# Down slabs split earlier, normalised rows on ScalarE, the inverse spread to the end, and four banks for the last four down blocks

## The chip, the cores and the metric

The kernel runs on one core of a Trainium2 chip. The metric is the device time of one execution in microseconds (us). The core has a matrix engine (TensorE, PE in the profile), two engines for element-wise work (VectorE, DVE, and ScalarE, ACT), GpSimd (POOL), and SyncE (SP), which here issues all transfers. Each engine works through its own instruction order and waits on semaphores for the others. Matrix products are written to PSUM, which has eight banks per partition; an element-wise engine has to read a bank out before it can be used again.

## The reference

`x` is 2048 x 448. Its rows are normalised, and the result is the sum of three things: `x` itself, a filter in the frequency domain, and a gated feed-forward block with 1792 hidden columns.

```python
xn = _layernorm(x, axis=-1)                       # (x - mean) / sqrt(var + 1e-5)
# A: X = rfft2(xn) * (w_r + 1j * w_i);  y = irfft2(X)
# B: gate = xn @ W_gate; up = xn @ W_up
#    h = gate * (gate > 0) * up;  y = h @ W_down
return x + _A_ref(xn, A_w_r, A_w_i) + _B_ref(xn, B_W_gate, B_W_up, B_W_down)
```

## The kernel before

**Numbers in two parts.** TensorE multiplies f16 numbers. Every f32 operand is therefore split in two f16 parts, a high and a low one, after scaling, and a product is made of three: high by high, high by low, low by high. ACT makes the high part (a scaled copy) and DVE the low one (the operand minus the high part). This holds for the normalised rows, the weights, the hidden values `h` and the operands of the Fourier transforms.

**Rows and chunks.** The 2048 rows are 16 tiles `n2` of 128; the four tiles with the same `n2 % 4` are a chunk `q` of 512 rows. The chunks are taken in the order 0, 2, 1, 3.

**The feed-forward block sets PE's order.** The 1792 hidden columns are 14 slabs `f` of 128, in groups of 5, 5 and 4. For each group, each chunk and each slab there is a gate/up unit `("gu", g, f, q)`: 20 matmuls of 512 columns and two half passes, into two banks of the tile `gu`, of which there are two, so four banks in all. Then `gu_post` reads it out in four operations that alternate between ACT and DVE: `gu_relu` (line 765), `gu_times` (769), which is the last to read the banks, `gu_hi` (773) and `gu_lo` (777). When a group's slabs are done for a chunk, four down units `("dn", g, n2)` follow, one for each tile of rows: `dn_mm` (796) runs three matmuls of 448 columns for each slab into one of two banks `dn`, and `dn_post` (802) adds the scaled result to `xy`, where the output is gathered. Down units are placed a little after their chunk, behind the next pair of gate/up units. The last four have nothing behind which to stand and come at the very end.

**The slabs of the weights** are prepared on the way. For a down slab these are `load_wd`, `wd_sq` (squares, ACT, line 186), `wd_sum` (sum over partitions, POOL), `wd_scale` (ten tiny DVE operations, up to line 706), `wd_hi` (ACT, 710) and `wd_lo` (DVE, 714). `sched(gslot(s, n), ...)` hangs them on the unit that is `n` gate/up units ahead of `s`, the last gate/up unit before the group's first down block.

**The background.** The Fourier work and the normalisation of chunks 1 and 3 form one list `bg` with a cost in us of DVE for each step. `run_bg` hands out steps while there is credit; each unit brings as credit a share of its time less what it costs DVE itself (`room`). The share is found by halving an interval so that the credit of the units from `RAMP` to `last_gu` is just the list's cost. The normalisation of a tile in the list is `ln_norm`: `ln_xn` (290) makes the row, `ln_hi` (299) its high part, `ln_copy` moves pieces, and `ln_lo` follows. The inverse transform is the end of the list: per tile `i_swap`, `i_pair`, `i_quad` (599 to 604), `i_hi` (611), `i_lo` (617), `i_sdft` (PE, 627), `i_pq` (632), `i_pqlo` (636), `i_ddft` (PE, 646) and `i_acc` (651), which adds to `xy`. Its two products use the two banks `fx`.

**The order of the instructions.** Apart from the opening, whose order is written out by hand, a scheduler puts each engine's instructions in order ahead of the run: among those that are ready in its own reckoning it takes the one with the highest priority. Priority is the order in the program, raised for `gu_post` and `dn_post` (by 400) and for the weights (by 200). On the chip an engine keeps that order, so an instruction that has to wait holds those behind it. A tile of rows is stored when both its sums are in: `store` acts at its second call.

Of the kernel before, what the change touches and what calls it, by code (L numbers as in the profile page):

```python
# [10 lines left out]
F32 = mybir.dt.float32  # L11
BF16 = mybir.dt.bfloat16
U32 = mybir.dt.uint32
AF = mybir.ActivationFunctionType
OP = mybir.AluOpType
AX = mybir.AxisListType

S, D, F = 2048, 448, 1792
# [5 lines left out]
GROUPS = [5, 5, 4]  # L24
# [120 lines left out]
def tile_gfnet_reglu(ctx: ExitStack, tc: tile.TileContext, x, xr, wgu, wd, wf, ident, c_fd, c_fm, c_im, c_row, c_id,  # L145
                     out):
    nc = tc.nc
    V, A, P, G = nc.vector, nc.scalar, nc.tensor, nc.gpsimd

    main = ctx.enter_context(tc.tile_pool(name="main", bufs=1))  # L150
    psum = ctx.enter_context(tc.tile_pool(name="psum", bufs=1, space=bass.MemoryType.PSUM))

    def mt(shape, dt, name, bufs=1):
        return main.tile(shape, dt, name=name, bufs=bufs)
# [6 lines left out]
    ov = out.rearrange("(n p) d -> p n d", n=16)  # L161
    wdv = wd.rearrange("(f p) d -> f p d", p=128)

    xy = mt([128, 16, D], F32, "xy")
# [11 lines left out]
    dsc = mt([128, len(GROUPS)], F32, "dsc")  # L176
# [33 lines left out]
    xr_t, xr_b = {}, {}  # L210
# [44 lines left out]
    rst = {}  # L255
# [19 lines left out]
    xn, tt, xn_b = {}, {}, {}  # L275
# [7 lines left out]
        tt[n2] = tts[state.setdefault("tn", 0) % 4]  # L283
        state["tn"] += 1

    def ln_xn(n2):
        xn_b[n2] = free.pop(0)
        xn[n2] = xn_b[n2].rearrange("p g c k -> p (g c k)")[:, 0:D]
        r, _, mean = rst[n2 % 4, n2 // 4]
        V.tensor_scalar(xn[n2], xr_t[n2], mean, r, op0=OP.subtract, op1=OP.mult)  # L290

    def ln_hi(n2, fused=False):
        new_tt(n2)
        o = tt[n2].rearrange("p a b -> p (a b)")[:, 0:D]
        r, nm, _ = rst[n2 % 4, n2 // 4]
        if fused:
            A.activation(o, xr_t[n2], AF.Identity, scale=r, bias=nm)
        else:
            A.activation(o, xn[n2], AF.Copy)  # L299

    def ln_copy(n2):
        t = tt[n2]
        G.tensor_copy(t[:, 7, 0:48].rearrange("p (a b) -> p a b", b=16), t[:, 0:3, 112:128])  # L303
        G.tensor_copy(t[:, 7, 64:128], t[:, 3, 0:64])

    def ln_norm(n2):
        ln_xn(n2)
        ln_hi(n2)
        ln_copy(n2)
        free.append(xr_b.pop(n2))  # L310
# [344 lines left out]
    wt, wdt, wsc = {}, {}, {}  # L655
# [61 lines left out]
    hps, ht = {}, {}  # L717
# [25 lines left out]
    def gu_unit(f, q, mate):  # L743

        gs, cs = (0, 1), slice(0, 512)
        if (f, q) in opened:
            gu_full(f, q, gs, cs, False, True)
            return
        gu_open(f, q)
        gu_full(f, q, gs, cs, True, False)  # L750
        gu_halves(f, q, mate)
# [33 lines left out]
    dps = {}  # L785
    stored = set()

    def dn_mm(fs, n2):
        q, j = n2 % 4, n2 // 4
        js = slice(128 * j, 128 * (j + 1))  # L790
        ps = psum.tile([128, 512], F32, name="dn", bufs=2)
        n = 3 * len(fs)
        i = 0
        for f in fs:
            for a, b in ((0, 0), (0, 1), (1, 0)):
                last["P"] = P.matmul(ps[:, 0:D], ht[f, q][:, a, js], wdt[f][:, b, :], start=(i == 0),  # L796
                                     stop=(i == n - 1)).ins
                i += 1
        dps[n2] = ps

    def dn_post(g, n2):
        last["V"] = V.scalar_tensor_tensor(xy[:, n2, :], dps[n2][:, 0:D], dsc[:, g:g + 1], xy[:, n2, :],  # L802
                                           op0=OP.mult, op1=OP.add).ins

    def store(n2):

        if n2 in stored:
            nc.sync.dma_start(ov[:, n2, :], xy[:, n2, :])
        stored.add(n2)
# [7 lines left out]
    def add(cost, fn, *a):  # L817
        bg.append((cost, PE_US.get(fn.__name__, 0.0), fn, a))

    def ln_chunk(q):  # L820
        for j in range(4):
            add(0.79, ln_stats, q, j)
        add(0.0, ln_sd, q)
        add(0.7, ln_rstd, q)
        n = [q + 4 * j for j in (0, 2, 1, 3)]
        for t in range(4 + 2):
            for st, (c, fn) in reversed(list(enumerate(((0.51, ln_norm), (0.78, ln_lo), (0.0, ln_dma))))):
                i = t - st
                if 0 <= i < 4:
                    add(c, fn, n[i])  # L830
        marks["T", q] = len(bg)
# [108 lines left out]
    def bg_item(fn, a):  # L940

        if "P" in last:
            with tc.issue_after(last["P"]):
                fn(*a)
        else:
            fn(*a)

    def run_bg(until=None, amount=0.0):
        credit[0] += amount
        while pos[0] < len(bg) and (credit[0] > 0 if until is None else pos[0] < until):  # L950
            c, p, fn, a = bg[pos[0]]
            bg_item(fn, a)
            pos[0] += 1
            credit[0] -= c - load[0] * p


    groups, f0 = [], 0
# [4 lines left out]
    units, pend = [], []  # L962
# [17 lines left out]
    def sched(i, fn, *a):  # L980
        at.setdefault(max(i, -1), []).append((fn, a))

    gus = [i for i, u in enumerate(units) if u[0] == "gu"]
    gpos = {i: n for n, i in enumerate(gus)}

    def gslot(i, back):
        n = gpos[i] - back
        return gus[n] if n >= 0 else -1

    for f in groups[1] + groups[2]:  # L990
        s = first[f]
# [15 lines left out]
    for g, fs in enumerate(groups):  # L1007
        s = max(i for i in gus if i < first["dn", g])
        if g:
            for i, f in enumerate(fs):  # L1010
                sched(gslot(s, 4), wd_sq, i, f)
            sched(gslot(s, 4), wd_sum, len(fs))
            sched(gslot(s, 3), wd_scale, g, fs)
            for i, f in enumerate(fs):
                sched(gslot(s, 2 - i // 2), wd_hi, i, f)
                sched(gslot(s, 2 - i // 2), wd_lo, i, f)
            for i, f in enumerate(fs):
                sched(gslot(s, 14 - i), load_wd, f)

# [17 lines left out]
    for c, q in enumerate(CHUNKS[:2]):  # L1037
# [3 lines left out]
        for j in range(4):  # L1041
            n2 = q + 4 * j
# [7 lines left out]
    q = CHUNKS[0]  # L1050
# [50 lines left out]
        return max(0.0, share * took(units[i]) - fixed(i))  # L1101


    last_gu = max(gus) - 6
    lo, hi = 0.3, 1.2
    for _ in range(40):
        m = (lo + hi) / 2
# [5 lines left out]
    @contextmanager  # L1113
    def after(i):
        k = max(0, len(anchors) - 1 - i)
        with tc.issue_after(anchors[k]), tc.issue_after(act_anchors[k]):
            yield

    for i, u in list(enumerate(units))[len(groups[0]):]:
        is_gu = u[0] == "gu"  # L1120
        if is_gu:
            _, g, f, q = u
            run_bg(until=marks["T", q])
            gu_unit(f, q, (mates.get(u) or (0, 0, None, None))[2:])
        else:
            _, g, n2, _ = u
            dn_mm(groups[g], n2)
        with after(LAG):
            for fn, a in at.get(i, []):
                with tc.high_priority(offset=200):  # L1130
                    fn(*a)
            for v in units[i + 1:i + 1 + AHEAD]:
                if v[0] == "gu":
                    run_bg(until=marks["T", v[3]])
            run_bg(amount=room(i, load[0]) if i >= RAMP else 0.0)
        if is_gu:
            with tc.high_priority(offset=400):
                gu_post(f, q)
        else:
            with tc.high_priority(offset=400):  # L1140
                dn_post(g, n2)
            if g == len(groups) - 1:
                store(n2)
        anchors.append(last["V"])
        act_anchors.append(last["A"])
    run_bg(until=len(bg))


_ORDER = ["x", "xr", "wgu", "wd", "wf", "ident", "c_fd", "c_fm", "c_im", "c_row", "c_id"]
# [43 lines left out]
```

## Time and profile before

| | |
|---|---|
| median of 3 runs | 452.71 us (451.13 to 453.31) |
| the profiled execution | 451.96 us, span 450.2 us |
| PE busy | 437.9 us (97%) |
| DVE busy | 390.3 us (87%) |
| ACT busy | 181.4 us (40%) |
| POOL busy | 30.8 us (7%) |
| DMA | 39.54 MB, mean 88 GB/s |

The span runs from the first to the last instruction; the execution's own time holds 1.8 us more. Busy PE means that a matmul is in flight; matmuls overlap, so the time of one in a row is longer than its distance to the next. In a row of the timeline stand start, duration, engine, line, operation, output and inputs, shapes and how many alike follow each other; in brackets at the end stands the idle time before it and what ended that.

### The profile page before, as it was taken

What the parts mean: (1) busy time and instruction counts of PE and PEld (TensorE: products, weight loads), DVE (VectorE), ACT (ScalarE), POOL (GpSimd) and SP (SyncE); (2) the same over time, 40 slices, a digit from 0 to 9 for tenths busy, and PEclk for the clock granted to TensorE, in tenths of its full rate; (3) what the DMA queues carried; (4) which work ended last, traced back from release to release, by engine and by line L of the source; (5) the groups of instructions that cost most, each with busy time, mean ns of one, the idle gap of its engine ahead of it and who ended that gap; (6) DMA issues with size and microseconds to landing.
All of it is one profiled execution on the core that took longest, in us unless ns stands there. A gap on an engine that the chain in (4) does not pass through costs nothing.

```text
span 450.2 us, 7332 instructions
## 1 busy us (share of the span) xinstructions
PE 437.9 (97%) x2613; PEld 218.1 (48%) x2613; DVE 390.3 (87%) x963; ACT 181.4 (40%) x390; POOL 30.8 (7%) x77
## 2 busy tenths in 40 slices
PE   6999999999999999999999999999998999999996
PEld 2544644455555444444444444444454555655642
DVE  5999798968979898999999999998999997987432
ACT  5896233632455583153133533244244243134120
POOL 3220020500000120000000100000000000000000
PEclk9999999999999999999999999999999999999999
DMA  7828994400001452340320300002020211111202
GB/s 251 320 67 244 326 336 93 78 18 22 2 1 66 136 183 72 93 145 21 103 64 4 90 31 1 1 1 72 28 78 28 83 45 50 66 55 34 103 21 82
DMA packets 37612, 39.54 MB, mean 88 GB/s; under 512 B 16534, under 2 KB 33480, under 8 KB 37576
## 3 DMA queue, kind: packets, MB, share of 16 engines
q1 hardware_dynamic: 37576, 39.09, 27.9%
q8 instruction: 20, 0.33, 0.3%
q14 instruction: 16, 0.13, 0.1%
HBM read 24.38 MB, written 3.67 MB: 62 GB/s over the span
## 4 chain that ended last, share of the span: by engine, by line
PE 54%; DVE 35%; DMA 5%; issue 3%; ACT 1%; SPq 1%; DVEq 0%; ACTq 0%
PE gu L728 28%; PE dn L796 16%; DVE g L769 3%; DMA sw<-y 3%; DVE h L777 3%; DVE xy L802 2%; PE fx L358 2%; PE fx L627 2%; DVE y L500 2%; PE fx L395 2%; DVE y L499 2%; PE fx L646 2%; DVE y L401 2%; DVE y L402 2%; PE gu L735 2%
## 5 line engine op out<-in xcount | busy, mean ns | idle before, releaser
L728 PE MATMUL gu<-T,wt 128*128 128x512 f16 (+1 forms) x1140 | 254.8, 375 | 0.5 <-DVE g L769 0.5
L728 PEld LDWEIGHTS <-wt 128*128 128x128 f16 x1140 | 108.8, 98 | 129.1 <-issue 9.2
L796 PE MATMUL dn<-wdt,h 128*128 128x448 f16 x672 | 136.6, 352 | 0.9 <-DVE xy L802 0.6
L796 PEld LDWEIGHTS <-h 128*128 128x128 f16 x672 | 65.1, 98 | 63.1 <-issue 2.3
L765 ACT ACTIVATE g<-gu 128x512 f32<-128x512 f32 x56 | 33.1, 590 | 83.3 <-PE gu L735 55.7
L773 ACT ACTIVATE h<-g 128x512 f16<-128x512 f32 x56 | 35.0, 626 | 65.7 <-DVE g L769 65.6
L769 DVE SCALAR_TENSOR_TENSOR g<-gu,g 128x512 f32<-128x512 f32 x56 | 38.3, 684 | 8.1 <-ACT g L765 8.0
L777 DVE TENSOR_TENSOR h<-g,h 128x512 f16<-128x512 f32 x56 | 38.3, 685 | 5.8 <-ACT h L773 5.4
L802 DVE SCALAR_TENSOR_TENSOR xy<-dn,dsc,xy 128x448 f32<-128x448 f32 x48 | 32.4, 679 | 10.5 <-PE dn L796 10.5
L678 ACT ACTIVATE wt<-wst,wsc 128x512 f16<-128x512 f32 x28 | 19.1, 714 | 14.0 <-DVE wsc L196 14.0
L611 ACT ACTIVATE vt<-y,fsc 128x456 f16<-128x456 f32 x16 | 10.7, 669 | 26.2 <-issue 8.9
L682 DVE SCALAR_TENSOR_TENSOR wt<-wst,wsc,wt 128x512 f16<-128x512 f32 x28 | 20.4, 743 | 0.1
L189 POOL PARTITION_ALL_REDUCE wm<-wm x15 | 8.1, 539 | 169.1 <-ACT junk L186 163.6
L735 PE MATMUL gu<-T,wt 64*128 64x512 f16 x112 | 17.0, 381 | 1.7 <-DVE g L769 1.6
L186 ACT ACTIVATE junk<-wst 128x512 bf16<-128x512 f32 x28 | 17.4, 620 | 0.6 <-DMA wst<-in_wgu 0.5
L532 DVE TENSOR_TENSOR y<-y,sw 128x228 f32<-128x228 f32 x32 | 12.4, 389 | 5.0 <-DMA sw<-y 3.6
L651 DVE SCALAR_TENSOR_TENSOR xy<-fx,fsc,xy 128x448 f32<-128x448 f32 x16 | 10.8, 679 | 6.8 <-PE fx L646 6.7
L402 DVE TENSOR_TENSOR y<-y,y 128x456 f32<-128x456 f32 x22 | 13.9, 630 | 2.8 <-DMA row<-y 2.2
L386 ACT ACTIVATE Xh<-X 128x456 f16<-128x456 f32 x16 | 9.3, 578 | 15.6 <-DVE X L384 10.9
L401 DVE TENSOR_TENSOR y<-y,y 128x456 f32<-128x456 f32 x22 | 13.8, 628 | 0.3
L627 PE MATMUL fx<-im,vt 128*128 128x128 f16 x192 | 13.4, 219 | 0.7 <-DVE pgh L636 0.7
L303 POOL COPY tt<-tt 128x48 f16<-128x48 f16 x16 | 9.5, 591 | 56.4 <-ACT tt L299 51.1
(122 smaller groups left out, 458.1 us busy)
## 6 DMA issues: line engine op xcount, KB each, us to landing
sw<-y SPq DMA_DIRECT2D x64, 112.2 KB
wst<-in_wgu SPq DMA_DIRECT2D x28, 256.0 KB
wf<-in_wf SPq DMA_DIRECT2D x16, 228.0 KB
y<-in_xr SPq DMA_DIRECT2D x16, 224.0 KB
xy<-in_x SPq DMA_DIRECT2D x16, 224.0 KB
out<-xy SPq DMA_DIRECT2D x16, 224.0 KB
wdst<-in_wd SPq DMA_DIRECT2D x14, 224.0 KB
fm<-in_c_fm SPq DMA_DIRECT2D x4, 256.0 KB
```

Of the source, the lines that this page charges most:

```text
L401: V.tensor_tensor(t, a, b, op=OP.add)
L402: V.tensor_tensor(b, a, b, op=OP.subtract)
L627: P.matmul(o, v[:, h, w], m[:, c, :], start=(i == 0), stop=(i == 2), skip_group_check=True)
L682: V.scalar_tensor_tensor(w[:, 4:8, :], st, sc, w[:, 0:4, :], op0=OP.mult, op1=OP.subtract)
L728: last["P"] = P.matmul(hps[f, q][:, g, cs], wt[f, g][:, a, :], Tq[q][:, b, cs], start=(start and i == 0), stop=(stop and i == len(seq) - 1 ...
L735: m = P.matmul(hps[f, q][:, g, 0:512], wt[f, g][rows, 7, :], Tq[q][rows, b, :], start=start, stop=not start).ins
L765: last["A"] = A.activation(g1s[f, q], hps[f, q][:, 0, :], AF.Relu, scale=2.0 ** -22).ins
L769: last["V"] = V.scalar_tensor_tensor(g1, hps[f, q][:, 1, :], 2.0 ** -22, g1, op0=OP.mult, op1=OP.mult).ins
L773: A.activation(ht[f, q][:, 0, :], g1s[f, q], AF.Copy)
L777: V.tensor_tensor(h[:, 1, :], g1s.pop((f, q)), h[:, 0, :], op=OP.subtract)
L796: last["P"] = P.matmul(ps[:, 0:D], ht[f, q][:, a, js], wdt[f][:, b, :], start=(i == 0), stop=(i == n - 1)).ins
L802: last["V"] = V.scalar_tensor_tensor(xy[:, n2, :], dps[n2][:, 0:D], dsc[:, g:g + 1], xy[:, n2, :], op0=OP.mult, op1=OP.add).ins
```

## The change

Five edits.

1. **Down slabs.** Squares and sum go from 4 to 8 gate/up units ahead of `s`, the scales from 3 to 6, and the splits from two slabs per unit at 2, 1 and 0 units ahead to one slab per unit at 5, 4, 3, 2 and 1 ahead.
2. **Normalised rows.** In the background (eight tiles, chunks 1 and 3) `ln_xn` runs on ACT as one activation with scale and bias. `ln_rstd` makes the bias there, one tiny DVE operation for each chunk. The costs in the list follow: 0.51 becomes 0, 0.7 becomes 0.75.
3. **The inverse.** `last_gu`, up to which credit is counted, goes from six to two units ahead of the last gate/up unit.
4. **The last four down blocks** leave the loop. `dn_tail` takes four banks, the two `dn` and the two `fx`, runs the matmuls of all slabs but the last for all four blocks, then those of the last slab.
5. **The last block** has the matmuls of its last slab, its sum and its store in two halves of 224 columns.

```diff
-    def ln_xn(n2):
+    def ln_xn(n2, act=False):
         xn_b[n2] = free.pop(0)
         xn[n2] = xn_b[n2].rearrange("p g c k -> p (g c k)")[:, 0:D]
-        r, _, mean = rst[n2 % 4, n2 // 4]
-        V.tensor_scalar(xn[n2], xr_t[n2], mean, r, op0=OP.subtract, op1=OP.mult)
+        r, nm, mean = rst[n2 % 4, n2 // 4]
+        if act:
+            A.activation(xn[n2], xr_t[n2], AF.Identity, scale=r, bias=nm)
+        else:
+            V.tensor_scalar(xn[n2], xr_t[n2], mean, r, op0=OP.subtract, op1=OP.mult)
...
     def ln_norm(n2):
-        ln_xn(n2)
+        ln_xn(n2, True)
...
+    def dn_tail(fs, ns):
+
+        ps = [psum.tile([128, 512], F32, name="dn", bufs=2) if i < 2 else fx() for i in range(4)]
+        cut = [(slice(0, D),)] * 3 + [(slice(0, D // 2), slice(D // 2, D))]
+        for end, p, n2, cs in [(False, p, n2, cut[0]) for p, n2 in zip(ps, ns)] + [(True, *e) for e in zip(ps, ns, cut)]:
+            q, j = n2 % 4, n2 // 4
+            js = slice(128 * j, 128 * (j + 1))
+            for c in cs:
+                for f in fs[-1:] if end else fs[:-1]:
+                    for a, b in ((0, 0), (0, 1), (1, 0)):
+                        P.matmul(p[:, c], ht[f, q][:, a, js], wdt[f][:, b, c],
+                                 start=(not end and f == fs[0] and a + b == 0), stop=(end and a == 1),
+                                 skip_group_check=True)
+            dps[n2] = p
+        for n2, cs in zip(ns, cut):
+            for c in cs:
+                V.scalar_tensor_tensor(xy[:, n2, c], dps[n2][:, c], dsc[:, len(GROUPS) - 1:len(GROUPS)], xy[:, n2, c],
+                                       op0=OP.mult, op1=OP.add)
+                nc.sync.dma_start(ov[:, n2, c], xy[:, n2, c])
...
-        add(0.7, ln_rstd, q)
+        add(0.75, ln_rstd, q, (0, 1, 2, 3), True)
...
-            for st, (c, fn) in reversed(list(enumerate(((0.51, ln_norm), (0.78, ln_lo), (0.0, ln_dma))))):
+            for st, (c, fn) in reversed(list(enumerate(((0.0, ln_norm), (0.78, ln_lo), (0.0, ln_dma))))):
...
             for i, f in enumerate(fs):
-                sched(gslot(s, 4), wd_sq, i, f)
-            sched(gslot(s, 4), wd_sum, len(fs))
-            sched(gslot(s, 3), wd_scale, g, fs)
+                sched(gslot(s, 8), wd_sq, i, f)
+            sched(gslot(s, 8), wd_sum, len(fs))
+            sched(gslot(s, 6), wd_scale, g, fs)
             for i, f in enumerate(fs):
-                sched(gslot(s, 2 - i // 2), wd_hi, i, f)
-                sched(gslot(s, 2 - i // 2), wd_lo, i, f)
+                sched(gslot(s, 5 - i), wd_hi, i, f)
+                sched(gslot(s, 5 - i), wd_lo, i, f)
...
-    last_gu = max(gus) - 6
+    last_gu = max(gus) - 2
...
-    for i, u in list(enumerate(units))[len(groups[0]):]:
+    for i, u in list(enumerate(units))[len(groups[0]):-4]:
...
     run_bg(until=len(bg))
+    dn_tail(groups[-1], [u[2] for u in units[-4:]])
```

## The prediction

> **What bounds the kernel now.** I read the page first, then who TensorE (PE) waits for, then the timeline around each wait, and last the busy time of each engine by stretches.
>
> ```profile
> span 450.2 us, 7332 instructions
> PE 437.9 (97%) x2613; PEld 218.1 (48%) x2613; DVE 390.3 (87%) x963; ACT 181.4 (40%) x390; POOL 30.8 (7%) x77
> ```
> ```profile
> PE gu L735 <- DVE g L769: 1.6, 1, 1.6
> PE fx L627 <- DVE pgh L636: 0.7, 1, 0.7
> PE fx L329 <- DVE tt L314: 0.6, 2, 0.4
> PE dn L796 <- DVE xy L802: 0.6, 1, 0.6
> PE fx L329 <- ACT wt L678: 0.5, 1, 0.5
> PE gu L728 <- DVE g L769: 0.5, 1, 0.5
> PE dn L796 <- ACT wdt L710: 0.3, 1, 0.3
> ```
>
> The second fence is the list of PE's waits (who, for whom, us in total, times, longest). PE is busy 97% of the span, so a change can win only the pauses left in its stream: 4.8 us in these rows, 1.1 of them (L329) in the opening, which the change leaves alone. The question is which of the others it ends and what new ones it makes.
>
> ```profile
> 275.00:325.00 50.00, 49.54 (x247) 22.47 (x246) 47.59 (x117) 17.16 (x33) 2.19 (x3) 1.00 0.06 19
> ...
> 375.00:431.00 56.00, 56.00 (x457) 32.87 (x455) 41.34 (x90) 15.52 (x27) 0.00 (x0) 1.00 0.19 65
> ```
>
> The columns are stretch, length, then PE, PE's weight loads, VectorE (DVE), ScalarE (ACT), POOL. From 275 to 325 us DVE is full as well (47.59 of 50 us); from 375 us it has air. A small thing put into DVE's or ACT's order in the middle can therefore reach PE; at the end it hardly can.
>
> **The down slabs, the largest term.** This is the second split, that of group 2, in the timelines of ACT, DVE and PE, and last the first split in PE's.
>
> ```profile
> 334.77 2.35 ACT L710 ACTIVATE wdt<-wdst,wds 128x448 f16<-128x448 f32 x4 [6.03 <-DVE wds L706]
> 337.03 0.57 ACT L765 ACTIVATE g<-gu 128x512 f32<-128x512 f32 x1
> ```
> ```profile
> 335.52 2.46 DVE L714 SCALAR_TENSOR_TENSOR wdt<-wdst,wds,wdt 128x448 f16<-128x448 f32 x4
> 337.90 0.68 DVE L769 SCALAR_TENSOR_TENSOR g<-gu,g 128x512 f32<-128x512 f32 x1
> ```
> ```profile
> 327.17 4.48 PE L728 MATMUL gu<-T,wt 128*128 128x512 f16 x20
> 331.48 0.83 PE L627 MATMUL fx<-im,vt 128*128 128x128 f16 x12
> 332.15 4.48 PE L728 MATMUL gu<-T,wt 128*128 128x512 f16 x20
> 336.47 0.61 PE L646 MATMUL fx<-idc_t,pgh 114*128 114x112 f16 x9
> 338.64 0.61 PE L735 MATMUL gu<-T,wt 64*128 64x512 f16 x4 [1.56 <-DVE g L769]
> ...
> 340.46 0.73 PE L627 MATMUL fx<-im,vt 128*128 128x128 f16 x10 [0.74 <-DVE pgh L636]
> ```
> ```profile
> 191.63 0.54 PE L796 MATMUL dn<-wdt,h 128*128 128x448 f16 x2 [0.34 <-ACT wdt L710]
> ```
>
> The unit whose 20 matmuls began at 327.17 was done at 331.65, and its relu (L765) could have run. But ACT works in order, and ahead of the relu stood the split (L710), which waited 6.03 us for the scales, ten tiny operations that DVE threads into its full order. Then came four slabs at once on ACT (2.35 us) and on DVE (2.46 us), and the product that frees the bank (L769) ran only at 337.90. PE, through with the next unit's 20 matmuls and nine of the inverse at 337.08, stood still, and again at 340.46 for the inverse, whose DVE work had slipped behind the same burst. At 191 us a down block waited for its slab itself.
>
> A row of idle understates the loss: the 20 matmuls of 432.15 (rows of the end, below) are shown as 4.49 us, though the next matmul starts 4.33 us later, so 0.16 us goes on top of each. The three waits are 0.34 + 1.56 + 0.74 + 3 x 0.16 = 3.12 us. After the change the squares and scales stand four and three gate/up units earlier, and the slabs go one per unit, five to one units ahead of the first block, not two per unit and two to none ahead. A single slab puts 0.65 us in ACT's order and 0.68 in DVE's, against 2.35 and 2.46. No instruction is added. Three things move along. The squares (four or five on ACT) now share units with the gate/up slabs' squares and splits; ACT has 17.16 of 50 us busy there, so I price them at nothing, but a relu behind them would be held as one was behind the splits. The sum over partitions on POOL moves with them; POOL is 7% busy. And with eight slab buffers, five of them live, the last slabs must wait for the old group's last four blocks, which stand before them in the order. The waits of 191 us and of 336 us lose their cause: I take the whole 3.12 us, bounds 0 and 3.12.
>
> **Normalised rows on ACT.** Eight rows move; rows by form:
>
> ```profile
> L290 DVE TENSOR_SCALAR y<-y,mv,rs 128x448 f32<-128x448 f32 x16 | 7.6, 507 | 0.1
> ...
> L297 ACT ACTIVATE tt<-y,rs 128x448 f16<-128x448 f32 x4 | 3.0, 748 | 1.0 <-DVE rs L271 1.0
> ...
> L271 DVE SCALAR_TENSOR_TENSOR rs<-mv,rs 128x2 f32<-128x2 f32 x2 | 0.3, 160 | 0.1
> ```
>
> DVE loses 8 x 0.507 and gains two bias products of 0.16: 3.7 us less busy. ACT gains 8 operations with scale and bias, 0.748 each as in L297: 6.0 us. They fall behind the opening and before the first split of 191 us, where no wait of the list above stands, so the path gets 0; if ACT's extra time did reach PE it would cost up to 6.0 us, if DVE were the bound there it would gain up to 3.7. New is that the ACT row waits for DVE's bias with the relus queued behind it, where before the copy of the row waited for L290 in the same place.
> The Trainium skill (ScalarE: Activation LUTs, Rules for kernel authors) says that add and multiply belong on VectorE, not ScalarE. The rows agree on the single operation (507 against 748 ns); by that rule the sum would be worse by the difference.
>
> **The inverse spread to the end.** The loop that spends the credit can be gone through with its own costs. The background's cost falls from 282.0 to 278.0 (8 x 0.51 out, 2 x 0.05 in), the units that share it gain one gate/up and three down units, and the share falls from 1.081 to 1.048: some 3% less DVE work per unit in the full stretch. One wait there has only DVE's load as cause:
>
> ```profile
> 292.57 3.61 PE L728 MATMUL gu<-T,wt 128*128 128x512 f16 x16 [0.46 <-DVE g L769]
> ```
>
> It is 0.46 + 0.16 = 0.62 us; I take half, 0.3, bounds 0 and 0.62.
> The price is at the end.
>
> ```profile
> 409.27 0.67 DVE L651 SCALAR_TENSOR_TENSOR xy<-fx,fsc,xy 128x448 f32<-128x448 f32 x1
> ...
> 430.05 1.27 DVE L651 SCALAR_TENSOR_TENSOR xy<-fx,fsc,xy 128x448 f32<-128x448 f32 x2 [1.64 <-PE fx L646]
> ```
>
> In the plan the last steps of the inverse were handed out after unit 92 and now after unit 96. From 409.27 to 430.05 its last sums (L651) come in four steps, 5.2 us each, since each waits for one of two fx banks. By the plan the row that stood at unit 91 moves to 93 and the next from 92 to 95: two steps later, so the last sum falls near 430.7 + 10.4 = 441.1 on the old clock.
>
> **The four banks.** PE's and DVE's timelines of the end, and the store's issue on SP (ns):
>
> ```profile
> 432.15 4.49 PE L728 MATMUL gu<-T,wt 128*128 128x512 f16 x20
> 436.48 4.70 PE L796 MATMUL dn<-wdt,h 128*128 128x448 f16 x24
> 441.76 4.70 PE L796 MATMUL dn<-wdt,h 128*128 128x448 f16 x24 [0.59 <-DVE xy L802]
> ```
> ```profile
> 441.03 1.27 DVE L802 SCALAR_TENSOR_TENSOR xy<-dn,dsc,xy 128x448 f32<-128x448 f32 x2 [1.65 <-PE dn L796]
> ...
> 446.50 0.69 DVE L802 SCALAR_TENSOR_TENSOR xy<-dn,dsc,xy 128x448 f32<-128x448 f32 x1 [1.59 <-PE dn L796]
> ```
> ```profile
> L808 SPq DMA_DIRECT2D out<-xy x16: 332/335/457, 350.3 to 447.2; - x16
> ```
>
> The old tail has one wait, 0.59 us for a dn bank. The new one runs 36 matmuls of the first three slabs, then 9 of the last slab for three blocks and 6 of half width (half the time, an estimate). One of full width takes (4.70 - 0.16)/24 = 0.189 us. So 45 x 0.189 + 6 x 0.10 = 9.1 us from 436.48: PE's last matmul starts at 445.5, and DVE, which follows with 0.61 us per block, does the last half (0.4 us, an estimate: little over half of 0.69) by 446.75 instead of 447.19. Gain 0.4 us. Bounds 0 and 0.6. The store and the close behind it take 450.2 - 447.19 = 3.0 us and are kept: SP issues five stores for four, 0.34 us each at 0.6 us of spacing, so none queues. The last unit's halves (four operations, near 2.9 us) hide behind the 36 matmuls, 6.8 us.
> Two of the four banks are the inverse's. Its two late steps bring their own matmuls behind the last gate/up unit: 12 of L627 at 0.67 us (331.48 to 332.15) and 36 of L646 at 0.05 each (nine in 0.61 less 0.16), 2.5 us, so that unit ends near 434.0; with 18 matmuls in the dn banks PE has work until 439.9, and the first fx bank is free near 441.1. That is a pause of up to 1.2 us, unless six matmuls of the last slab (1.1 us) are ordered ahead: I take 0.5.
> The Trainium skill (PSUM — Partial Sum Buffer, PSUM bank collisions raise a hardware error) asks to guard by bank, not by address; by that the first half of the last block is not read while the second is written, and the halves gain on DVE and the store alone, as summed above. No run here shows it.
>
> **Sum.** -3.12 - 0.3 - 0.4 + 0.5 = -3.3 us on the profiled execution's 451.96 (span 450.2 and 1.8 around it): 448.7. That execution lies 0.75 us under the median of 452.71, so the forecast is **449.4 us**.
>
> **Rivals.** First, the block on ACT comes back in the new place. Scales and first slab are still one unit apart, and the scales now share DVE with two gate/up slab halves per unit. With one slab the product would come 3.1 us (the wait from 331.65 to 334.77), 0.65, 0.57 and 0.68 us after the matmuls' end, 5.0 us and more after it, where PE needs it within 5.4 (331.65 to 337.08): just in time. If the scales come 1 us later at each of the two places, 2.1 us are lost again: 451.5. For it: DVE's 47.59 of 50; against: three units of lead. Chance 0.20.
> Second, on the other side: the inverse ends too late. After the last sum PE still has two blocks, 18 + 3 matmuls and 6 halves, 4.55 us, then 1.1 for DVE and 3.0 to the span's end. Each further step of 5.2 us beyond 441.1 is lost nearly whole: one makes 449.4 + 5.2 = 454.6, two some 459. It decides from about 446 us on the old clock. For it: the plan's end moves four units, over 11 us of PE; against: DVE has 41.34 of 56 us busy there, and an idle PE shortens the steps. Chance 0.14.
> Third, ACT's longer rows reach PE: 8 x (0.748 - 0.507) = 1.9 us, 451.3. Against: no wait there. Chance 0.04. The Trainium skill's rule above would have this case.
> Fourth, the change does not do what it says: the instruction order is made by priorities among what is ready, and the slabs could be placed late all the same: 452.7. Chance 0.05.
>
> **How the numbers follow.** The forecast has 0.57; its own range is 447.0 (the median less 3.12 + 0.62 + 0.4, and less the 1.6 us by which the lowest run lies under it) to 450.4. Faster by over 0.5% (about what a measurement of this kernel can tell from no change, here 2.3 us) is this case; within 0.5% are the first, third and fourth rivals, 0.29; slower is the second, 0.14. Upwards the range takes in the fourth rival with the 0.6 us by which the highest run lies over the median, 453.4; what is left out is the second rival and little below.
>
> **What would show it.** Right: no wait of PE for L710, L735 or L627 in the middle, L710 in single rows from about 165 and 308 us on, PE waits beyond the start under 2 us, last L651 at 436 to 439, the final matmuls without a pause over 1 us. Wrong: a relu that stands behind a split for over 5 us, PE idle before the third bank, or new waits of PE between 60 and 175 us.

## The result and the profile after

| | before | after |
|---|---|---|
| median | 451.71 us (6 runs beside the after, 451.13 to 453.31) | 449.12 us (6 runs, 448.19 to 449.44) |
| ratio to before | | 0.9929 [0.9911, 0.9947] |
| profiled execution | 451.96 us, span 450.2 us | 449.44 us, span 447.6 us |

The change makes the kernel faster by 0.7% [0.5%, 0.9%]; the medians lie 2.6 us apart. The forecast was 449.4 us. The experiments below show that the total came out as forecast while three of its terms did not. Executions at a granted TensorE clock of 0.994 to 0.996 took longer (the kernel before 452.21 to 454.04 us, against 450.48 to 452.48 at 0.998 to 1.000), so a median also depends on how many of each it holds.

The page of the kernel after, then who PE waits for:

```profile
span 447.6 us, 7353 instructions
PE 437.9 (98%) x2616; PEld 218.8 (49%) x2616; DVE 387.2 (87%) x958; ACT 186.7 (42%) x398; POOL 28.8 (6%) x77
```
```profile
PE dn L1049 <- POOL warm L1106: 3.6, 1, 3.6
PE gu L738 <- DVE g L772: 1.4, 1, 1.4
PE fx L332 <- ACT wt L681: 0.4, 1, 0.4
PE dn L799 <- DVE xy L805: 0.3, 1, 0.3
PE gu L738 <- DVE wt L685: 0.2, 1, 0.2
```

Lines up to the row's stand three further down in this kernel (L772 is the product that was L769, L805 was L802, L738 the half passes of L735), the matmuls and sums of the new tail are L818 and L824. The 3.6 us for POOL belong to the opening and stand in every kernel here; the prediction's list leaves them out. The waits for the slab (L710) and for the inverse (L627) are gone. Left in the middle are 1.4 us for a product and 0.3 us for a down bank. The 1.4 us are not a new place: counted through PE's matmuls, the half passes that wait at 336.16 are the same ones that waited 1.56 us at 338.64 in the kernel before. What holds their product up is another thing now. The stretches (length, then PE, weight loads, DVE, ACT, POOL):

```profile
275.00:325.00 50.00, 49.71 (x248) 22.69 (x247) 46.60 (x117) 20.69 (x43) 1.75 (x3) 1.00 0.06 19
375.00:431.00 56.00, 56.00 (x437) 31.85 (x435) 45.12 (x104) 16.82 (x29) 0.00 (x0) 1.00 0.19 63
```

DVE has 1.0 us less in the middle (46.60 against 47.59) and 3.8 us more late (45.12 against 41.34): the inverse has moved. The slabs on ACT are single rows, and the relu waits for PE's matmuls, not behind a split:

```profile
159.10 0.66 ACT L713 ACTIVATE wdt<-wdst,wds 128x448 f16<-128x448 f32 x1
...
182.66 0.67 ACT L713 ACTIVATE wdt<-wdst,wds 128x448 f16<-128x448 f32 x1 [5.06 <-PE dn L799]
...
326.32 0.65 ACT L713 ACTIVATE wdt<-wdst,wds 128x448 f16<-128x448 f32 x1
330.21 0.60 ACT L768 ACTIVATE g<-gu 128x512 f32<-128x512 f32 x1 [3.23 <-PE gu L731]
```

The pause of the half passes in DVE's timeline, then in PE's:

```profile
315.92 0.40 DVE L535 TENSOR_TENSOR y<-y,sw 128x228 f32<-128x228 f32 x1 [2.65 <-DMA y<-row]
...
329.45 0.40 DVE L535 TENSOR_TENSOR y<-y,sw 128x228 f32<-128x228 f32 x1 [1.42 <-DMA sw<-y]
...
331.57 0.67 DVE L717 SCALAR_TENSOR_TENSOR wdt<-wdst,wds,wdt 128x448 f16<-128x448 f32 x1
...
335.43 0.68 DVE L772 SCALAR_TENSOR_TENSOR g<-gu,g 128x512 f32<-128x512 f32 x1
```
```profile
336.16 0.61 PE L738 MATMUL gu<-T,wt 64*128 64x512 f16 x4 [1.40 <-DVE g L772]
```

The relu was done at 330.81, but the product that frees the bank began at 335.43. DVE was busy all that time: it works its list in order, and between 330.67 and 335.43 stand 13 operations of the inverse, one down sum and one split (L717). It came to them late because it had stood still for 2.65 and 1.42 us, both times for a DMA: the transformed row that the inverse's pairs need, and the swapped copy. Between the row's last step and this first use stands one DVE operation; in the kernel before there stood four. What the row's wait is made of is shown below, under "Spread and rows".

### The profile page after: what moved, and what is told of

The parts are those of the page before. It is cut to its first block, busy times and chain, and to the rows that moved or that the text cites. A ratio compares the mean times of both kernels' runs of the same rounds, so it can differ in the third digit from the quotient of the medians.

```text
span 447.6 us, 7353 instructions
## 1 busy us (share of the span) xinstructions
PE 437.9 (98%) x2616; PEld 218.8 (49%) x2616; DVE 387.2 (87%) x958; ACT 186.7 (42%) x398; POOL 28.8 (6%) x77
## 4 chain that ended last, share of the span: by engine, by line
PE 52%; DVE 38%; DMA 3%; issue 3%; ACT 2%; POOL 1%; SPq 1%; DVEq 0%; ACTq 0%; POOLq 0%
PE gu L731 26%; PE dn L799 12%; DVE g L772 3%; DVE h L780 3%; DVE wt L685 3%; DVE xy L805 2%; PE fx L630 2%; PE fx L649 2%; DVE y L502 2%; DVE y L503 2%; DVE y L405 2%; DVE y L404 2%; DMA sw<-y 2%; DVE y L427 2%; PE gu L738 2%
## 5 line engine op out<-in xcount | busy, mean ns | idle before, releaser
L799 PE MATMUL dn<-wdt,h 128*128 128x448 f16 x624 | 127.1, 352 | 0.3 <-DVE xy L805 0.3
L799 PEld LDWEIGHTS <-h 128*128 128x128 f16 x624 | 60.3, 98 | 57.7 <-issue 1.1
L772 DVE SCALAR_TENSOR_TENSOR g<-gu,g 128x512 f32<-128x512 f32 x56 | 38.2, 682 | 4.2 <-ACT g L768 4.2
L805 DVE SCALAR_TENSOR_TENSOR xy<-dn,dsc,xy 128x448 f32<-128x448 f32 x44 | 29.8, 678 | 6.2 <-PE dn L799 6.2
L189 POOL PARTITION_ALL_REDUCE wm<-wm x15 | 9.3, 617 | 181.9 <-ACT junk L186 161.8
L654 DVE SCALAR_TENSOR_TENSOR xy<-fx,fsc,xy 128x448 f32<-128x448 f32 x16 | 10.9, 679 | 11.0 <-PE fx L649 10.9
L738 PE MATMUL gu<-T,wt 64*128 64x512 f16 x112 | 17.0, 381 | 1.6 <-DVE g L772 1.4
L392 DVE TENSOR_TENSOR Xh<-X,Xh 128x456 f16<-128x456 f32 x16 | 9.9, 626 | 5.8 <-ACT Xh L389 5.7
```

The costliest lines, as they stand in the source:

```text
L738: m = P.matmul(hps[f, q][:, g, 0:512], wt[f, g][rows, 7, :], Tq[q][rows, b, :], start=start, stop=not start).ins
L772: last["V"] = V.scalar_tensor_tensor(g1, hps[f, q][:, 1, :], 2.0 ** -22, g1, op0=OP.mult, op1=OP.mult).ins
```

## What the runs have in common: one sum

From the starts of consecutive matmuls in PE's timeline one can read off each pause in full (the idle time shown plus the 0.16 us of the prediction). The table takes all pauses over 0.25 us behind the opening, with the time at which PE goes on, and beside it how much earlier or later than in the kernel before the opening ends (the wait of the first half passes for their weights; no edit touches the opening, so I take this as scatter between executions). "Sum" is 450.2 plus the opening's shift plus the change in pauses from 4.51. "Edits" are numbered as in the change.

| kernel | edits | pauses (us at us) | opening | sum | span |
|---|---|---|---|---|---|
| before | none | 0.50 at 192, 0.62 at 293, 1.73 at 339, 0.91 at 340, 0.75 at 442: 4.51 | | | 450.2 |
| after | 1 to 5 | 0.45 at 320, 1.56 at 336: 2.01 | -0.16 | 447.5 | 447.6 |
| slabs only | 1 | 0.39 at 292, 0.75 at 439: 1.14 | -0.06 | 446.8 | 447.1 |
| no slabs | 2 to 5 | 1.31 at 192, 0.62 at 332: 1.93 | -0.87 | 446.8 | 447.1 |
| spread only | 3 | none: 0 | -0.65 | 445.0 | 445.1 |
| tail only | 4, 5 | 0.40, 0.59, 1.70, 0.90 at before's first four: 3.59 | -0.30 | 449.0 | 449.3 |
| spread, tail | 3 to 5 | 0.35 at 437: 0.35 | -0.45 | 445.6 | 445.8 |
| spread, rows | 2, 3 | 1.33 at 192, 0.72 at 332, 0.58 at 440: 2.63 | +0.03 | 448.4 | 448.4 |
| spread, slabs | 1, 3 | none: 0 | -0.18 | 445.5 | 445.6 |
| no rows | 1, 3 to 5 | 0.35 at 437: 0.35 | -0.47 | 445.6 | 445.8 |
| rows at the old cost | 1, 3 to 5, and of 2 the operations | 0.28 at 204, 0.35 at 438: 0.63 | -0.42 | 445.9 | 446.2 |
| costs only | 1, 3 to 5, and of 2 the figures | 1.29 at 335: 1.29 | -0.58 | 446.4 | 446.6 |
| row early | 1 to 5, the row's last steps earlier | 0.53 at 297: 0.53 | -0.36 | 445.9 | 446.1 |
| slabs in pairs | 1 in part | 0.85 at 292, 0.72 at 396, 0.75 at 439: 2.32 | -0.38 | 447.6 | 447.7 |

The sum gives every span within 0.35 us. So PE's pauses and the opening account for the spans of these kernels, and each edit can be judged by the pauses that it ends and makes. Each row is one execution. The opening's scatter of up to 0.9 us is as large as some of the differences; where spans are compared below, the pauses decide.

## Experiments

The kernels were timed in three groups, each beside the kernel before: it took 451.72 us beside the first four below, 451.35 beside the three after them and the row's steps earlier, 452.26 beside the other four. Ratios are to these, with their 95% intervals.

**Slabs only.** The kernel before with edit 1.

```diff
-                sched(gslot(s, 4), wd_sq, i, f)
+                sched(gslot(s, 8), wd_sq, i, f)
...
-                sched(gslot(s, 2 - i // 2), wd_hi, i, f)
+                sched(gslot(s, 5 - i), wd_hi, i, f)
...
```

> The kernel before with the first edit alone (squares, scales and splits of the down slabs earlier, one slab per unit). Theory A, the prediction's: the slabs held the relu and the bank, so the three waits (191, 336 and 339 us) go and the time falls by 3.1 us, to 0.993 of before. Rival B: the trace after the whole change still has a pause of 1.4 us where the inverse starts, with no slab burst in front of it; the order of VectorE at that place is late anyway, so only the wait of 191 us and part of the rest go: 0.5 to 1.5 us, 0.997 to 0.999.

449.11 us, 0.9936 [0.9916, 0.9956]. PE's waits:

```profile
PE dn L1026 <- POOL warm L1083: 3.6, 1, 3.6
PE dn L796 <- DVE xy L802: 0.6, 1, 0.6
PE fx L329 <- ACT wt L678: 0.4, 1, 0.4
PE gu L728 <- DVE g L769: 0.2, 1, 0.2
```

The three waits that I put down to the slabs are gone, the others are there: 2.6 us of the 3.12 forecast by the medians, 3.1 by the pauses. By itself the edit does what it was costed for.

**All but the slabs.** The kernel after with the old places of edit 1.

```diff
-                sched(gslot(s, 8), wd_sq, i, f)
+                sched(gslot(s, 4), wd_sq, i, f)
...
-                sched(gslot(s, 5 - i), wd_hi, i, f)
+                sched(gslot(s, 2 - i // 2), wd_hi, i, f)
...
```

> The whole change without its first edit: slabs as before, the other four edits kept. Theory A: 3.1 us of the gain are the slabs', so almost nothing is left, 0.999 to 1.001 of before, and the waits for the down split (a relu behind four slabs) are back in the trace. Rival B: the other edits hold half of the gain or more, 0.995 to 0.997.

449.37 us, 0.9939 [0.9918, 0.9959]: the whole change without what I took for nearly all of its gain is as fast as with it. PE's waits for a product are two, other than those of before:

```profile
PE gu L731 <- DVE g L772: 1.6, 2, 1.1
```

So the slabs are one way to end the old waits, and something else among the edits is another.

**Spread only.** The kernel before with edit 3.

```diff
-    last_gu = max(gus) - 6
+    last_gu = max(gus) - 2
```

> The kernel before with the third edit alone (credit counted to two units ahead of the last gate/up unit). The prediction's terms: 0.3 us less from the fuller stretch; the price for late banks does not arise, since the tail uses only its own two banks: 0.999 to 1.000. Rival: the lower share takes away the wait of 292 us and the late start of the inverse moves its pause too: 0.5 to 2 us less, 0.996 to 0.999. Rival on the other side: with the old slab bursts the later inverse meets them, up to 1 us more.

447.19 us (446.87 to 447.36), 0.9888 [0.9869, 0.9907]. This one number makes the fastest kernel of the study: 4.5 us under the kernel before, and its interval lies wholly below that of the whole change. PE's waits are three, all in the opening. In ACT's timeline the burst of four slabs is still there:

```profile
PE dn L1026 <- POOL warm L1083: 3.6, 1, 3.6
PE fx L329 <- ACT wt L678: 0.5, 1, 0.5
PE gu L735 <- DVE wt L682: 0.2, 1, 0.2
```
```profile
327.94 2.35 ACT L710 ACTIVATE wdt<-wdst,wds 128x448 f16<-128x448 f32 x4 [4.65 <-DVE wds L706]
330.20 0.57 ACT L765 ACTIVATE g<-gu 128x512 f32<-128x512 f32 x1
```

ACT waits for the scales 4.65 us instead of 6.03, and the relu behind the burst is in time. In the kernel before the last scale was done at 334.73, 3.1 us after the matmuls of the relu's unit (331.65); here it is done at 327.91, about 1.1 us ahead of them (20 matmuls from 324.73, at 4.33 us, are through at 329.06). So in the kernel before the pause needed both, the burst and a DVE that comes late to the scales. And at the end 24 of the inverse's matmuls now lie between two down blocks, so PE never asks for a bank that is not free:

```profile
432.87 2.81 PE L796 MATMUL dn<-wdt,h 128*128 128x448 f16 x14
435.52 1.35 PE L646 MATMUL fx<-idc_t,pgh 114*128 114x112 f16 x24
436.70 4.70 PE L796 MATMUL dn<-wdt,h 128*128 128x448 f16 x24
```

**Tail only.** The kernel before with edits 4 and 5.

```diff
-    for i, u in list(enumerate(units))[len(groups[0]):]:
+    for i, u in list(enumerate(units))[len(groups[0]):-4]:
...
+    dn_tail(groups[-1], [u[2] for u in units[-4:]])
```

> The kernel before with the fourth and fifth edit alone (last four down blocks in four banks, last block in halves). The inverse ends at 430.7 us here, so its banks are free. The prediction's term: 0.4 us less, 0.999. By the trace of the whole change, whose tail has no pause left: 0.75 us less, 0.998. If the store or the two halves cost more than they win: no change, 1.000.

451.76 us, 0.9997 [0.9978, 1.0016]: no gain in the median. In the trace the wait for the down bank at the end (0.75 us) is gone and all others are as before:

```profile
PE gu L735 <- DVE g L769: 1.5, 1, 1.5
PE fx L627 <- DVE pgh L636: 0.7, 1, 0.7
```

Some of it is given back: from the start of the last matmul to the end of the span it takes 4.3 us here, 4.1 before. What is left, about half a us, is inside the interval of 0.9 us to either side. The median hides it in part: six of its twelve executions had a granted clock of 0.994 or 0.995. The other six, at 0.998 and 0.999, have a median of 450.80 us, and the eleven of the kernel before at 0.998 to 1.000 one of 451.25, 0.45 us more.

**Spread and tail.** Edits 3, 4 and 5 without 1 and 2.

```diff
-    last_gu = max(gus) - 6
+    last_gu = max(gus) - 2
...
+    dn_tail(groups[-1], [u[2] for u in units[-4:]])
```

> The third edit (inverse spread to the end) with the tail in four banks, slabs and rows as before. The inverse ends late and holds two of the four banks: the prediction's price of up to 1.2 us would show here against the third edit alone (0.989): 0.990 to 0.992, with a pause of PE ahead of the third bank. If the tail costs nothing and its 0.75 us are still to be had: 0.987. If the late inverse already fills the pause of the old tail: 0.989.

447.82 us, 0.9916 [0.9900, 0.9932]; the interval overlaps that of the spread alone. The trace has one new pause, that of the third bank:

```profile
PE fx L815 <- DVE xy L651: 0.2, 1, 0.2
```

It is 0.35 us in full: the price foreseen for holding the inverse's banks. The spread alone has no bank wait at the end for four banks to remove, so only the price remains.

**Spread and rows.** Edits 2 and 3.

```diff
-    last_gu = max(gus) - 6
+    last_gu = max(gus) - 2
...
+            A.activation(xn[n2], xr_t[n2], AF.Identity, scale=r, bias=nm)
...
-        add(0.7, ln_rstd, q)
+        add(0.75, ln_rstd, q, (0, 1, 2, 3), True)
...
```

> The third edit with the rows on ScalarE alone. Theory C, with the rows' lower cost the background runs ahead and meets the row transfer without cover: VectorE waits over 2 us for it and PE pauses again, 1 to 2 us over the third edit alone, 0.991 to 0.993. Rival: the rows are free or help, 0.987 to 0.989.

450.20 us, 0.9971 [0.9960, 0.9983]. The rows take back 3 us of the spread's 4.5, and the intervals do not touch. PE's waits in the loop, and DVE's from 280 to 345 us:

```profile
PE gu L731 <- DVE g L772: 1.7, 2, 1.2
```
```profile
DVE y L535 <- DMA y<-row: 2.2, 1, 2.2
```

Neither is the old slab wait come back: at both places the relu was done long before (187.55 and 327.51), and the split stands behind it on ACT, not ahead of it. The products came late in DVE's order, at 191.76 and 331.72. The one at 331.72 follows the wait for the row. The one at 191.76 stands behind most of the scales' ten operations, which DVE begins 2.2 us later than in the spread alone (186.42 against 184.18); 0.74 us of that is a wait for a swapped copy at 184.66, the rest was not traced.

The row's wait has a part that is not DVE's. In this kernel as in the spread alone two DVE operations stand between the row's last step and its first use, but one waits 2.2 us and the other 0.2. SP issues the copies in order, and its rows show the difference, here and then in the spread alone:

```profile
312.45 0.70 SPq L530 DMA_DIRECT2D sw<-y  x1
313.24 3.08 SPq L592 DMA_DIRECT2D y<-row  x4
```
```profile
308.04 0.70 SPq L527 DMA_DIRECT2D sw<-y  x1
308.83 3.00 SPq L589 DMA_DIRECT2D y<-row  x4
```

The row was ready at 311.91 here and at 308.80 in the spread alone. Here SP still had swapped copies to issue, 0.7 us each, and came to the row 1.3 us later; there it came at once. The other 0.7 us between the two waits are no gain: in the spread alone DVE spends them waiting for ACT. From the issue to the first use it takes 2.3 us in both, and 2.2 to 2.35 us in all eleven kernels in which DVE waits for the row. In the whole change SP came 1.1 us after the row was ready.

**Spread and slabs.** Edits 1 and 3.

```diff
-    last_gu = max(gus) - 6
+    last_gu = max(gus) - 2
...
-                sched(gslot(s, 4), wd_sq, i, f)
+                sched(gslot(s, 8), wd_sq, i, f)
...
```

> The third edit with the early slabs alone. If gains of both add up beyond what the third edit has: nothing is left to win in the middle, since it has no pause there, so 0.989. If the slabs' moved work makes the pause of the whole change: 0.991 to 0.994.

447.20 us, 0.9902 [0.9886, 0.9918], no pause behind the opening: the same as the spread alone. Two edits that end the same waits are worth one of them.

**All but the rows.** The kernel after with edit 2 undone.

```diff
-        ln_xn(n2, True)
+        ln_xn(n2)
...
-        add(0.75, ln_rstd, q, (0, 1, 2, 3), True)
+        add(0.7, ln_rstd, q)
...
```

> The whole change without its second edit: rows on VectorE as before, with the old costs; slabs, spread and tail kept. If the second edit is what brings the pause of 334 us back, that pause goes and the time is that of the spread with the tail or with the slabs, 0.990 to 0.992 of before. Rival: the pause belongs to the slabs and the tail together, 0.993 as in the whole change.

447.71 us, 0.9901 [0.9883, 0.9919], 1.4 us under the whole change in the medians, though the two intervals still overlap. The pause of 336 us is gone; left is the price of the third bank. DVE waits for the row 0.6 us instead of 2.65:

```profile
DVE y L532 <- DMA y<-row: 0.6, 1, 0.6
```

So edit 2 costs something. It is two things: eight operations on another engine, and new figures in the list by which steps are handed out. The next two kernels part them.

**Rows on ACT at the old cost.** The kernel after, with the list's figures of before.

```diff
-        add(0.75, ln_rstd, q, (0, 1, 2, 3), True)
+        add(0.7, ln_rstd, q, (0, 1, 2, 3), True)
...
-            for st, (c, fn) in reversed(list(enumerate(((0.0, ln_norm), (0.78, ln_lo), (0.0, ln_dma))))):
+            for st, (c, fn) in reversed(list(enumerate(((0.51, ln_norm), (0.78, ln_lo), (0.0, ln_dma))))):
```

> The whole change with the old costs of the rows in the background list (0.51 and 0.7): the rows still run on ScalarE, only the credit loop reckons as before. Theory D: not the operation but the reckoning did it; with 4 us less in the list every later step shifts against the units, so that the transformed row comes right ahead of its first use. Then the pause goes: 0.990 to 0.992. Rival E: the operation itself did it, and the pause stays: 0.993.

448.44 us, 0.9913 [0.9897, 0.9929]. DVE's waits from 280 to 345 us:

```profile
DVE y L535 <- DMA y<-row: 0.8, 1, 0.8
```

The row is waited for 0.8 us and there is no pause at 336.

**New costs only.** The kernel after, with the rows on DVE as before, but the list's figures of edit 2. The background then brings 4 us more of DVE than it says.

```diff
-            A.activation(xn[n2], xr_t[n2], AF.Identity, scale=r, bias=nm)
...
-        add(0.75, ln_rstd, q, (0, 1, 2, 3), True)
+        add(0.75, ln_rstd, q)
```

> The converse: rows on VectorE as before, but with the new costs in the list (0 and 0.75), the rest of the whole change kept. Theory D: the pause and VectorE's wait of over 2 us for the row stay, 0.993 or, with 4 us of uncounted work on VectorE, up to 0.995. Rival E: they go, 0.990 to 0.992.

448.19 us, 0.9911 [0.9894, 0.9927]. PE's wait, and DVE's in the same stretch:

```profile
PE gu L735 <- DVE g L769: 1.1, 1, 1.1
```
```profile
DVE y L532 <- DMA y<-row: 2.4, 1, 2.4
DVE y L532 <- DMA sw<-y: 1.6, 1, 1.6
```

Both DMA waits of the kernel after are back, and the pause with them (1.29 us in full), without a single row on ACT. In the traces the pause goes with the figures, not with the engine: the four kernels with spread and new figures and the list's order unchanged wait 2.1 to 2.65 us for the row and pause at 332 to 336 us, the five with spread and old ones wait 0.2 to 0.8 us and do not. By their times these last two kernels cannot be told apart: 448.44 and 448.19 lie within each other's intervals, and both overlap the whole change and the change without rows. That the pause comes from the figures is shown; that it is all of the rows' cost in time is not.

**The row's steps earlier.** The kernel after; the end of the row's transform, six entries of the list (the expectation says nine), is put ahead of the last second and third stages instead of behind them, so that more work lies between the row and the pairs that need it. The row's last step then ends at 290.74 us instead of 312.55.

```diff
+        if i0 == 9:
+            add(0.1, wsq_fin)
+            add(0.8, wsq_scale)
+            for c, fn in zip(rows_us[4:], rows[4:]):
+                add(c, fn)
         if i0 > 1:
             back(ks[i0 - 2])
...
-    add(0.1, wsq_fin)
-    add(0.8, wsq_scale)
-    for c, fn in zip(rows_us[4:], rows[4:]):
-        add(c, fn)
```

> The whole change, with the scales of the filter and the last part of the row transform (nine steps of the background list) put ahead of the last second and third stages instead of behind them. Theory C: the pause of 1.4 us at 334 us comes from VectorE, which in its fixed order waits 2.65 us for the transfer of the transformed row and 1.42 for a swap and so has the product that frees the bank 4 us late. With some 8 us of stage work between the row and its first use that wait goes, the pause with it, and the time falls by 1.5 to 2 us against the whole change: 0.988 to 0.990 of before. Rival: the pause comes from the amount of work VectorE has there; it stays, and the time is that of the whole change, 0.993.

448.08 us, 0.9925 [0.9905, 0.9944]. The wait for the row is gone from DVE's list, that for the swap is not, and the pause of 336 us is gone with the row's; a smaller one (0.53 us in full) has come at 297 us:

```profile
PE gu L738 <- DVE g L772: 0.4, 1, 0.4
```
```profile
DVE y L535 <- DMA sw<-y: 1.7, 2, 1.4
```

The pause of 320 us is gone too. From the wait for the swapped copy to the product that frees the bank DVE has the same eighteen operations in the same order as in the whole change; they only start 3.1 us earlier (326.35 against 329.45). The row's wait therefore made the pause. The median is 1 us lower, but the ratio's interval does not tell it from the whole change.

**Slabs in pairs.** Edit 1 alone with its lead, but two slabs per unit as before.

```diff
-                sched(gslot(s, 2 - i // 2), wd_hi, i, f)
-                sched(gslot(s, 2 - i // 2), wd_lo, i, f)
+                sched(gslot(s, 5 - i // 2), wd_hi, i, f)
+                sched(gslot(s, 5 - i // 2), wd_lo, i, f)
...
```

> The kernel before with squares, scales and splits as early as in the first edit, but still two slabs per unit. If the lead alone ended the waits for the slabs: as the first edit alone, 0.9936. If single slabs matter (a pair puts 1.3 us ahead of a relu): a part of the waits at 191 and 336 us is left, 0.995 to 0.998.

449.55 us, 0.9941 [0.9926, 0.9956], as the single slabs. The waits of 192 and 339 us are gone here too; a bank wait at 292 has grown and one for the inverse has come at 396 us:

```profile
PE gu L728 <- DVE g L769: 0.7, 1, 0.7
PE dn L796 <- DVE xy L802: 0.6, 1, 0.6
PE fx L627 <- DVE pgh L636: 0.6, 1, 0.6
```

So it was the lead that ended the slab waits, not their splitting up. In the two traces the single slabs have 1.2 us less of pauses (1.14 against 2.32); the times do not tell the two apart.

## Why the prediction was right, and where it was not

The total was right, 449.4 against 449.12, and so was the direction. But that it came so close is luck, for errors of both signs cancelled. The fall was forecast at 3.3 us; the medians fell by 2.6 and the pauses by 2.50 (4.51 to 2.01). And the fall was taken from 452.71, a median of three; the six executions beside the result have 451.71. A fall 0.7 us too large from a start 1.0 us too high ends 0.3 us from the measured time. The fall itself is a sum of terms that miss, as follows.

**The slabs, -3.12: right alone, not as a term of a sum.** Alone they bring 2.6 us in the medians and 3.1 in pauses. With the spread they bring nothing (447.20 against 447.19). The failing step is the adding up: the same waits stood to be ended by another edit of the same change. What I called the cause, the burst on ACT, was only one of two conditions, and the largest of the three waits did not need it: in the whole change the same half passes wait 1.56 us in full (1.73 before) with no split ahead of the relu. Among the signs listed as right stood that PE would have no wait for L735 in the middle; that one did not come true.

**The spread, -0.3: the direction was right, the size off by more than a factor of ten.** I saw a lower share of DVE and gave it one wait that had "only DVE's load as cause", bound 0.62. The runs show that the slab waits, too, end with edit 3 alone (4.5 us of pauses gone), since DVE comes to the scales earlier, and that the late matmuls of the inverse fill the end where the down bank was waited for. The bound was wrong because I asked which wait had DVE as its sole cause, not which waits would still be there with DVE earlier. Whether the lower share does it, or the other order that comes with it, no run parts. The share alone does not decide: the loop of the list gives 1.081 for the kernel before, 1.058 for edit 3 alone and 1.048 with the figures of edit 2, and it is at 1.048 that the pauses of 332 to 336 us come.

**The rows, 0: wrong sign.** In the whole change they cost 1.4 us in the medians (1.66 in pauses), and on the spread alone 3.0 us (2.63). I weighed busy times (DVE 3.7 less, ACT 6.0 more) and looked for a wait where the rows stand. Both readings were right: DVE is 3.1 us less busy, ACT 5.3 more, and the new wait for the bias, which I named, is hidden:

```profile
L291 ACT ACTIVATE y<-y,rs 128x448 f32<-128x448 f32 x8 | 5.5, 749 | 4.9 <-DVE rs L271 4.9
```

What I left out is the other half of the edit. The figure 0.51 set to 0 shifts when every later step of the list is handed out, and the end of the row's transform comes to stand close ahead of the pairs that use it, with a DMA between them and other copies ahead of it on SP. The prediction counted the fall from 282.0 to 278.0 as less work only. The Trainium skill's rule (ScalarE: Activation LUTs, Rules for kernel authors) would have had the rows dearer by the difference of 749 and 507 ns. They were dearer, but the runs do not bear out that reason: the pause comes as well with the rows on DVE and only the figures changed.

**Four banks, -0.4, and their price, +0.5.** The price came true on the spread, 0.35 us of pause, and not in the whole change, where the order has the tail's matmuls among the inverse's and PE does not wait:

```profile
433.92 3.00 PE L818 MATMUL dn<-wdt,h 128*128 128x448 f16 x15
...
438.13 1.11 PE L818 MATMUL dn<-wdt,h 128*128 128x448 f16 x5
439.07 4.71 PE L818 MATMUL fx<-wdt,h 128*128 128x448 f16 x27
```

Beside the spread alone there was no gain to be had, as its row shows. Beside the spread with the rows there was: that kernel waits 0.58 us in full for a down bank at 440 us, and the kernel without the slabs, which differs from it by the tail alone, does not, so there the four banks are worth some 0.6 us of pause and cost nothing. The halves of the last block bring nothing:

```profile
437.55 1.47 DVE L654 SCALAR_TENSOR_TENSOR xy<-fx,fsc,xy 128x448 f32<-128x448 f32 x2 [1.95 <-PE fx L649]
...
443.82 0.81 DVE L824 SCALAR_TENSOR_TENSOR xy<-fx,dsc,xy 128x224 f32<-128x224 f32 x2 [1.59 <-PE fx L818]
```

PE's last matmul ends at 439.07 + 4.71 = 443.78. Both half sums start behind that, though the first half had its last matmul three earlier, 0.3 us before. The prediction's sum had only the last half, 0.4 us, behind PE; in fact both follow, 0.81 us where one operation of 0.69 stood. From the start of the last matmul to the end of the span it takes 4.1 us before and after. This is what the prediction's sentence from the Trainium skill (PSUM — Partial Sum Buffer, PSUM bank collisions raise a hardware error) foresaw: a guard by bank, under which the first half is not read while the second is written. The trace agrees. But the sum beside that sentence did not follow it, for under such a guard both halves come behind PE. The trace also shows what set the wait: of the six half-width matmuls only the last (start 443.53) raises the semaphore that the first half's sum waits for. The guard stands in the program; what the chip does without it no run shows.

**The end of the inverse.** The last L654 lies at 437.55 to 439.02, within 436 to 439 but for the last sum's end, and PE has 27 matmuls left: the second rival, the slower one, did not come about.

**The other rivals.** The split did not come back as a block on ACT (first rival), but the pause came back at the same half passes by another road: DVE's order, not ACT's. The list of signs had "a relu that stands behind a split"; the relu was free, and the product behind it was not. The wait of ACT for the old group's blocks (5.06 us at 182.66) was foreseen and costs nothing.

## What to carry to other kernels

A pause with two conditions can be ended from either side, so gains of edits that aim at the same pauses must not be added: for each stall ask which of the other edits would end it too. Where steps are handed out by a list of costs, changing a cost moves everything behind it; read it as a change of order, and look where a producer, a DMA and its consumer come to lie close together, and what the issuing engine has to issue before that DMA. And try the one-line edit alone: here it beat the whole change (0.9888 against 0.9929).

## What the runs showed of the hardware

Two things that I had not expected. The copies of the row and of the swap held DVE for up to 2.65 and 1.6 us, when no DVE operation of the whole change from 40 to 440 us takes more than 0.85. The row's copy took 2.2 to 2.35 us from its issue on SP to its first use, and lay ready for 0.03 to 1.33 us before SP issued it, behind other copies of 0.7 us each. And the opening, the same in all these kernels, ended up to 0.9 us apart (from -0.87 to +0.03 us against before, one execution of each kernel), so that a difference of spans under 1 us says nothing until its pauses are found.
